# A pair's last 64 queries as one block-diagonal product, with single buffers for the transposed q and k

## The chip, the cores and the metric

The kernel runs on one core of one Trainium2 chip. The metric is the device time of one execution in microseconds. The kernel before takes 1670.19 us (median of 3 runs, 1670.05 to 1670.26). All arithmetic is in 32-bit floats, and the granted clock of TensorE in the profiled run was 0.997 of full speed.

## What is computed

Attention with a threshold, followed by a Fourier mixing block:

```python
# q, k, v: (8, 8, 576, 64)   batch, heads, sequence, head size
scores = q @ k.T / 8
thresh = max(scores, axis=-1) - tau
scores = where(scores >= thresh, scores, -1e9)
attn   = exp(scores - max) / (sum + 1e-9)
x      = attn @ v                     # as (8, 576, 512)
u      = x + real(fft(fft(x, axis=1), axis=2))
un     = (u - mean(u)) / sqrt(var(u) + 1e-6)
out    = u + relu(un @ w_ch1) @ w_ch2 # 512 -> 2048 -> 512
```

The change concerns `scores` only.

## The kernel before, in words

**Pairs and steps.** Two heads of a batch make a pair: head j of the pair lies on partitions 64j to 64j + 63. There are 32 pairs, four in a batch. The 576 queries are taken in five steps (`NT = 5`): steps 0 to 3 have 128 queries of each head, and step 4 has the last 64 of both heads, one head on each half of the partitions.

**Loading and transposing a pair.** `load_pair` (L124 to L147) brings q and k of a pair into one buffer `qk` of nine slots of 128 rows. Slots 0 to 3 hold the first 512 queries, slots 4 to 7 hold 512 keys, slot 8 holds the last 64 queries above 64 keys. The second head's keys are loaded in another order: the last 64 keys first, then 0 to 511, so its weights later lie where the product with v wants them. `prep_in_parts` (L389 to L416) transposes the nine slots on TensorE, in three parts. Part one: four transposes `pq`, then VectorE scales them into `qT` (L399). Part two: four transposes `pk`, then ScalarE copies them into `kT` (L406). Part three: one transpose `pt` of slot 8, then VectorE scales its q half into the end of `qT` (L410), copies its k half to the end of `kT` (L413), and the next pair's load is issued. `qT` and `kT` have two buffers each, so that the next pair can be transposed while the present one is still in use.

**Scores.** `scores(i)` (L422 to L448) fills PSUM tiles `sc`, of which there are two. In steps 0 to 3 it does four products over 64 rows each (L433), in step 4 five products of 64 rows by 64 columns (L444): both heads write to one tile, head 1's on the lower half of the partitions, and since head 1's keys are rotated by 64, its second half of the keys takes two products:

```python
for j, c, c0, k0, w in (
    (0, 0, 0, 0, HALF), (1, 0, 0, 64, HALF), (0, 1, 0, HALF, HALF),
    (1, 1, 0, 64 + HALF, 512 - HALF), (1, 1, 512 - HALF, 0, 64),
):
    hp = slice(64 * j, 64 * j + 64)
    nc.tensor.matmul(sc[0][hp, c, c0 : c0 + w], qT[hp, 512:S], kT[hp, k0 : k0 + w], ...)
```

**Softmax.** `softmax(i)` takes the maxima on VectorE (L461), the exponential on ScalarE (L469), the threshold and the sum on VectorE (L477), and the division (L492, L496). The weights are then transposed on TensorE (L541, L560), copied by ScalarE into `e_t` (L548 to L564) and multiplied with v (L589).

**What sets the order.** In the first two batches (pairs 0 to 7) every engine keeps the order of writing. The first batch also converts the first weight matrix from 64-bit input and fills TensorE with dummy products (`busy`, L112). The second converts the second weight matrix (L298 to L320, on VectorE, ScalarE and GpSimd in turn; `advance` takes the stages one by one) and starts the Fourier mixing and the channel products. From batch 3 on only TensorE keeps the order of writing, and a scheduler orders the other engines. There, `fill()` puts pieces of the Fourier mixing (L692 to L713) and of the channel products (L822, L848, L926, L1090), up to a budget per slot, between the pieces of attention: three slots a step. In batches 2 to 8 the next pair's preparation is called in step 3: in one go in batch 2 (`second_batch`), and in batches 3 to 8 one part at a time, before, between and after the transposes of the weights. In batch 1 it is called in step 4 (`step`). All products' PSUM tiles other than `sc` share four banks (tag `mm`).

Of the kernel before, what the change touches and what calls it, by code (L numbers as in the profile page):

```python
# [9 lines left out]
FP32 = mybir.dt.float32  # L10
INT32 = mybir.dt.int32
UINT32 = mybir.dt.uint32
ALU = mybir.AluOpType
# [34 lines left out]
def kernel(  # L48
# [12 lines left out]
    nc = tc.nc  # L61
    B, H, S, D = q.shape
# [3 lines left out]
    NPAIR = H // 2  # L66
# [3 lines left out]
    HALF = S // 2  # L70
# [12 lines left out]
    const = ctx.enter_context(tc.tile_pool(name="const", bufs=1))  # L83
    sb = ctx.enter_context(tc.tile_pool(name="sb", bufs=2))
# [39 lines left out]
    def load_pair(n, queue=nc.sync):  # L124
        b, p = n // NPAIR, PAIRS[n % NPAIR]
        hs = [2 * p + (j + p) % 2 for j in range(2)]

        qk = sb.tile([128, 9, 2, D], FP32, tag="qk", bufs=1, name="qk_in")
        for j, h in enumerate(hs):
            nc.sync.dma_start(  # L130
                out=qk[:, 0:4, j, :], in_=q[b, h, 0:512, :].rearrange("(t p) d -> p t d", p=128)
            )
            nc.sync.dma_start(out=qk[0:64, 8, j, :], in_=q[b, h, 512:576, :])


        h = hs[0]
        queue.dma_start(
            out=qk[:, 4:8, 0, :], in_=k[b, h, 0:512, :].rearrange("(t p) d -> p t d", p=128)
        )
        queue.dma_start(out=qk[64:128, 8, 0, :], in_=k[b, h, 512:576, :])  # L140
        h = hs[1]
        queue.dma_start(out=qk[0:64, 4, 1, :], in_=k[b, h, 512:576, :])
        rows = k[b, h, 0:512, :].rearrange("(t r p) d -> p r t d", r=2, p=64)
        queue.dma_start(out=qk[64:128, 4:8, 1, :], in_=rows[:, 0])
        queue.dma_start(out=qk[0:64, 5:8, 1, :], in_=rows[:, 1, 0:3])
        queue.dma_start(out=qk[64:128, 8, 1, :], in_=rows[:, 1, 3])
        loaded[n] = qk  # L147

    def load_v(n):
# [21 lines left out]
    for u in range(2):  # L171
        for j in range(2):
            nc.gpsimd.memset(v_in[u][64 - 64 * j : 128 - 64 * j, 8 + j, :], 0.0)
    eps = const.tile([128, 1], FP32, name="eps")
    nc.vector.memset(eps[:], 1e-6)

# [3 lines left out]
    q_scale = const.tile([128, 1], FP32, name="q_scale")  # L180
    nc.vector.tensor_scalar(
        out=q_scale[:], in0=tau_t[:], scalar1=0.0, scalar2=SCALE, op0=ALU.is_ge, op1=ALU.mult
# [3 lines left out]
        out=below[:], in0=tau_t[:], scalar1=0.0, scalar2=-3.0e38, op0=ALU.is_lt, op1=ALU.mult  # L186
# [3 lines left out]
        out=tau_pos[:], in0=tau_t[:], scalar1=0.0, scalar2=-1.0, op0=ALU.max, op1=ALU.mult  # L190
# [82 lines left out]
    hs = const.tile([128, NJ * GT], FP32, name="hs")  # L273
# [115 lines left out]
    def prep_in_parts(n):  # L389


        qk = loaded.pop(n)
        qT = sb.tile([128, S], FP32, tag="qT", name="qT")
        kT = sb.tile([128, S], FP32, tag="kT", name="kT")

        pq = ps.tile([128, 512], FP32, tag="mm", bufs=4, name="pq")
        for t in range(4):
            nc.tensor.transpose(pq[:, 128 * t : 128 * t + 128], qk[:, t, :, :], ident[:, :])
        nc.vector.tensor_scalar(  # L399
            out=qT[:, 0:512], in0=pq[:, :], scalar1=q_scale[:, :], scalar2=None, op0=ALU.mult  # L400
        )
        yield
        pk = ps.tile([128, 512], FP32, tag="mm", bufs=4, name="pk")
        for t in range(4):
            nc.tensor.transpose(pk[:, 128 * t : 128 * t + 128], qk[:, 4 + t, :, :], ident[:, :])
        nc.scalar.copy(kT[:, 0:512], pk[:, :])  # L406
        yield
        pt = ps.tile([128, 512], FP32, tag="mm", bufs=4, name="pt")
        nc.tensor.transpose(pt[:, 0:128], qk[:, 8, :, :], ident[:, :])
        nc.vector.tensor_scalar(  # L410
            out=qT[:, 512:S], in0=pt[:, 0:64], scalar1=q_scale[:, :], scalar2=None, op0=ALU.mult
        )
        nc.vector.tensor_copy(kT[:, 512:S], pt[:, 64:128])  # L413
        heads[n] = (qT, kT, v_in[n % 2])
        if n + 1 < B * NPAIR:
            load_pair(n + 1)  # L416
# [6 lines left out]
    def scores(i):  # L423
        n, t = divmod(i, NT)
        qT, kT = heads[n][0:2]

        nh = 2 if t < 4 else 1
        sc = [ps.tile([128, 2, 512], FP32, tag="sc", name=f"sc{j}") for j in range(nh)]
        if t < 4:
            for c in range(2):  # L430
                for j in range(2):
                    hp = slice(64 * j, 64 * j + 64)
                    nc.tensor.matmul(  # L433
                        sc[j][:, c, 0:HALF], qT[hp, 128 * t : 128 * t + 128],
                        kT[hp, HALF * c : HALF * (c + 1)], start=True, stop=True,
                    )
        else:

            for j, c, c0, k0, w in (
                (0, 0, 0, 0, HALF), (1, 0, 0, 64, HALF), (0, 1, 0, HALF, HALF),  # L440
                (1, 1, 0, 64 + HALF, 512 - HALF), (1, 1, 512 - HALF, 0, 64),
            ):
                hp = slice(64 * j, 64 * j + 64)
                nc.tensor.matmul(  # L444
                    sc[0][hp, c, c0 : c0 + w], qT[hp, 512:S], kT[hp, k0 : k0 + w],
                    start=True, stop=True, skip_group_check=True,
                )
        steps[i] = (sc, nh)  # L448

# [866 lines left out]
    def second_batch(i):  # L1316

        nonlocal budget
        n, t = divmod(i, NT)
        first = i - per_batch  # L1320
        if first != 1:
            scores(i)
        if first == 0:

            transposed_weights(i - 1)
        softmax(i, None, lambda: (advance(first - 1), advance(first - 1)))
        chunks.pop(first - 1, None)
        transfers(first)
        fold_more()
        if first == 0:  # L1330
            weighted_values(n - 1, 1)
            scores(i + 1)
            column_means(LAST)
            copy_mean(LAST)
            folds.append(fold_rows(n - 1))
            while folds:
                fold_more()
            load_v(n + 1)
            start_batch(0)
            mix(3)  # L1340
            mix(3)
        elif first == 1:
            mix(3)
            transposed_weights(i - 1)
            mix(2)
            mirrored(LAST)
            for c, eng in ((1, nc.vector), (3, nc.vector), (0, nc.gpsimd), (2, nc.gpsimd)):
                less_mean(eng, LAST, c)
            advance(first)
            advance(first)  # L1350
        elif first == 2:
            mix(2)
            transposed_weights(i - 1)
            mix(2)
            weighted_values(n, 0)
            advance(first)
            advance(first)
        else:
            fill()
            transposed_weights(i - 1)  # L1360
            advance(first)
            advance(first)
            fill()
            if t == 3:
                prep_pair(n + 1)
            fill()
            if t == 2:
                weighted_values(n, 0)
            if t == 0:
                weighted_values(n - 1, 1)  # L1370
                folds.append(fold_rows(n - 1))
                load_v(n + 1)
        if first == 16:
            fold_halves(1)
        if first < 3:
            budget += 3 * per_slot
# [7 lines left out]
    by_hand.close()  # L1384
    ctx.enter_context(tc.manual_schedule(engines={mybir.EngineType.PE}))

    for i in range(2 * per_batch, total + 1):


        if i < total:  # L1390
            scores(i)
        n, t = divmod(i, NT)
        if t > 2:
            fold_more()
        nothing = iter(())
        prep = prep_in_parts(n + 1) if t == 3 and n + 1 < B * NPAIR else nothing
        weights = weights_in_parts(i - 1)
        next(prep, None)
        fill()
        next(weights, None)  # L1400
        fill()
        next(weights, None)
        next(prep, None)
        if i < total:
            softmax(i)
        fill()
        next(prep, None)
        if t == 2:
            weighted_values(n, 0)
        if t == 0:  # L1410
            while folds:
                fold_more()
            weighted_values(n - 1, 1)
            folds.append(fold_rows(n - 1))
            if n % NPAIR == 0:
                while folds:
                    fold_more()
            if n + 1 < B * NPAIR:
                load_v(n + 1)
        if i % per_batch == 0:  # L1420
            start_batch(i // per_batch - 1)
# [49 lines left out]
```

## Time and profile before

| | |
|---|---|
| time, median of 3 | 1670.19 us |
| span of the profiled run | 1669.6 us |
| TensorE busy | 1621.8 us, 97% |
| VectorE, ScalarE, GpSimd busy | 69%, 50%, 35% |
| L433, scores of steps 0 to 3 | 1024 passes, 168.6 us busy |
| L444, scores of step 4 | 320 passes, 38.2 us busy |
| L398, L405, L409, transposes of a pair | 288, 48.5 us busy |
| L399 / L406 / L410 / L413, one instruction | 741 / 592 / 274 / 211 ns |

A group's line gives the line of the code, engine, operation, result and operands, the shape, how many, their busy time, and the idle time of the engine before them with what ended it. A 32-bit product is recorded as two passes, so the 160 products of L444 count as 320; a transpose counts once. Matmuls are pipelined and their ends are modelled, so busy time adds up overlaps: what a group costs is better read from the distance between starts in the timeline. "PEld" is the loading of weights, which can run beside products. In the timeline the bracket at a line's end is the idle time of the engine ahead of it and what released it.

### The profile page before, as it was taken

How to read it: one execution, taken by the hardware profiler on the slowest of the kernel's cores; microseconds unless marked ns; L12 is line 12 of the kernel's file. 1: busy time of each engine (PE TensorE's matmuls, PEld its weight loads, DVE VectorE, ACT ScalarE, POOL GpSimd, SP SyncE). 2: the span in 40 equal slices, each digit the busy share in tenths (PEclk: the TensorE clock that was granted, in tenths of full speed). 3: DMA queues.
4: the chain of work that ended last, by engine and by line, in shares of the span. 5: the costliest groups of instructions: out<-in, count | busy, mean ns of one | idle time of the engine just before them, and what ended most of it. 6: DMA issues, size and time to landing. Idle time of an engine off the chain costs nothing.

```text
span 1669.6 us, 28885 instructions
## 1 busy us (share of the span) xinstructions
PE 1621.8 (97%) x10826; PEld 1273.6 (76%) x10826; DVE 1146.0 (69%) x2518; ACT 837.9 (50%) x1817; POOL 581.9 (35%) x779
## 2 busy tenths in 40 slices
PE   8998899999999999999999999999999999999998
PEld 4555555577887888878888778887878788889998
DVE  6887785567757686857566858686677768664454
ACT  5775675544455454545354546454646455532111
POOL 5674562041321442134332143213242244215232
PEclk9999999999999999999999999999999999999999
DMA  5423222100010101000101010111001010000000
GB/s 157 121 55 110 73 73 56 30 20 21 19 39 15 29 15 42 23 28 8 28 22 35 10 34 15 42 22 29 22 16 42 22 32 4 14 1 13 14 13 13
DMA packets 130384, 57.48 MB, mean 34 GB/s; under 512 B 121123, under 2 KB 121125, under 8 KB 130246
## 3 DMA queue, kind: packets, MB, share of 16 engines
q1 hardware_dynamic: 128854, 55.35, 12.3%
q8 instruction: 86, 1.41, 0.4%
q14 instruction: 52, 0.43, 0.1%
q10 hardware_dynamic: 1392, 0.30, 0.1%
HBM read 46.02 MB, written 9.44 MB: 33 GB/s over the span
## 4 chain that ended last, share of the span: by engine, by line
PE 76%; DVE 15%; ACT 7%; issue 2%; POOL 1%; DVEq 0%; ACTq 0%; POOLq 0%
PE ph L926 23%; PE po L1090 18%; PE pv L589 8%; PE sc L433 7%; PE pw L560 5%; PE po L848 3%; DVE e L477 3%; DVE neg L461 2%; ACT e L469 2%; DVE hs L1051 2%; PE sc L444 2%; PE ph L822 1%; PE py L692 1%; PE pa L709 1%; PE pn L782 1%
## 5 line engine op out<-in xcount | busy, mean ns | idle before, releaser
L469 ACT ACTIVATE e<-sc,neg 128x576 f32<-128x576 f32 x288 | 212.6, 738 | 238.1 <-DVE neg L461 237.4
L461 DVE TENSOR_REDUCE neg<-sc 128x1 f32<-128x576 f32 x288 | 206.2, 750 | 171.4 <-PE sc L433 158.5
L477 DVE SCALAR_TENSOR_TENSOR e<-sc,thr,e 128x576 f32<-128x576 f32 x288 | 229.7, 811 | 57.5 <-ACT thr L473 54.2
L1090 PE MATMUL po<-w,hs 128*128 128x256 f32 x1024 | 246.3, 383 | 0.5 <-DVE u L804 0.5
L1090 PEld LDWEIGHTS po<-w,hs 128*128 128x128 f32 x1024 | 186.0, 190 | 33.6 <-issue 11.2
L926 PE MATMUL ph<-u_t,w 128*128 128x128 f32 x1536 | 187.2, 276 | 0.0
L926 PEld LDWEIGHTS ph<-u_t,w 128*128 128x128 f32 x1536 | 178.7, 192 | 4.4 <-issue 3.3
L560 PE MATMUL pw<-ident,e 128*128 128x128 f32 x1152 | 169.5, 274 | 10.4 <-ACT kT L406 2.7
L562 ACT COPY e_t<-pw 128x512 f32<-128x512 f32 x256 | 148.9, 596 | 59.8 <-PE pw L560 59.3
L433 PE MATMUL sc<-kT,qT 64*128 64x288 f32 x1024 | 168.6, 429 | 6.8 <-DVE e L477 6.0
L560 PEld LDWEIGHTS pw<-ident,e 128*128 128x128 f32 x1152 | 134.2, 141 | 29.3 <-issue 4.3
L935 DVE TENSOR_TENSOR hs<-ph,hs 128x512 f32<-128x512 f32 x160 | 106.9, 685 | 71.4 <-PE ph L926 46.8
L433 PEld LDWEIGHTS sc<-kT,qT 64*128 64x128 f32 x1024 | 93.2, 186 | 69.3 <-issue 37.2
L926 PE MATMUL ph<-t_u,s_w 128*128 128x128 f32 x1024 | 126.0, 276 | 2.2 <-POOL t_u L900 1.8
L804 DVE SCALAR_TENSOR_TENSOR u<-po,rstd,u 128x256 f32<-128x256 f32 (+1 forms) x164 | 75.4, 484 | 73.8 <-PE po L1090 71.9
L926 PEld LDWEIGHTS ph<-t_u,s_w 128*128 128x128 f32 x1024 | 119.4, 192 | 5.3 <-issue 2.6
L1090 PE MATMUL po<-hs,s_tile 128*128 128x256 f32 x512 | 122.1, 382 | 0.0
L496 ACT ACTIVATE e<-e,den 128x576 f32<-128x576 f32 x96 | 75.0, 781 | 67.4 <-DVE den L489 66.7
L1090 PEld LDWEIGHTS po<-hs,s_tile 128*128 128x128 f32 x512 | 93.6, 190 | 13.6 <-issue 2.1
L943 ACT ACTIVATE hs<-hs 128x512 f32<-128x512 f32 x112 | 69.4, 631 | 63.9 <-DVE hs L935 63.9
L622 POOL TENSOR_TENSOR half<-x 128x287 f32<-128x287 f32 x48 | 40.4, 862 | 125.5 <-ACT x L595 70.7
L1086 POOL TENSOR_TENSOR hs<-hs,s_tile 128x512 f32<-128x512 f32 x32 | 42.3, 1323 | 117.5 <-PE po L1090 113.8
(199 smaller groups left out, 2905.8 us busy)
## 6 DMA issues: line engine op xcount, KB each, us to landing
hs<-in_moe_w_ch_dram SPq DMA_DIRECT2D x23, 512.0 KB, 4.4
out_dram<-u SPq DMA_DIRECT2D x36, 256.0 KB, 2.2
qk_in<-in_q_dram SPq DMA_DIRECT2D x64, 128.0 KB, 2.3
v_in<-in_v_dram SPq DMA_DIRECT2D x64, 128.0 KB, 2.4
qk_in<-in_k_dram SPq DMA_DIRECT2D x31, 128.0 KB, 2.5
w<-in_moe_w_ch_dram SPq DMA_DIRECT2D x6, 512.0 KB, 8.4
qk_in<-in_k_dram SPq DMA_DIRECT2D x31, 64.0 KB, 2.3
stage<-in_moe_w_ch_dram SPq DMA_DIRECT2D x3, 512.0 KB, 3.8
```

Of the source, the lines that this page charges most:

```text
L433: nc.tensor.matmul(sc[j][:, c, 0:HALF], qT[hp, 128 * t : 128 * t + 128], kT[hp, HALF * c : HALF * (c + 1)], start=True, stop=True,)
L461: nc.vector.tensor_reduce(out=neg[:, j : j + 1], in_=sc[j][:, :, 0:HALF], axis=AXIS_XY, op=ALU.max, negate=True,)
L469: nc.scalar.activation(out=ej, in_=sc[j][:, :, 0:HALF], func=ACT.Exp, bias=neg[:, j : j + 1], scale=1.0)
L477: nc.vector.scalar_tensor_tensor(out=ej, in0=sc[j][:, :, 0:HALF], scalar=thr[:, j : j + 1], in1=ej, op0=ALU.is_ge, op1=ALU.mult, accum_out ...
L496: nc.scalar.activation(out=e[:, S : 2 * S], in_=e[:, S : 2 * S], func=ACT.Copy, scale=den[:, 1:2])
L560: nc.tensor.transpose(pw[:, c, :], e[:, c0 : c0 + 128], ident[:, :])
L562: nc.scalar.copy(e_t[:, 4 * j : 4 * j + 4, qs], pw[:, :, :])
L589: nc.tensor.matmul(pv[64 * j : 64 * j + 64, 0:m], vt[:, 2 * c + j, :], e_t[:, 4 * j + c, 0:m] if c < 4 else ends[:, 0:m], start=(c == 0), ...
L804: nc.vector.scalar_tensor_tensor(out=u, in0=product, scalar=self.rstd[:, t : t + 1], in1=u, op0=ALU.mult, op1=ALU.add,)
L926: nc.tensor.matmul(banks[name][:, 128 * q : 128 * q + 128], left[c][:, 512 * part + 128 * q : 512 * part + 128 * q + 128], right[c], start ...
L935: nc.vector.tensor_tensor(out=to, in0=bank, in1=to if other is None else other, op=ALU.add)
L1090: nc.tensor.matmul(bank[:, 0 : DM // 2], left[p], right[p], start=start and p == 0, stop=p == NK - 1, skip_group_check=True,)
```

## The change

The scores of step 4 become two products over all 128 rows. A constant tile `q_ends` of 128x128, cleared once, holds head 0's last 64 queries in its upper left quarter and head 1's in its lower right quarter. Multiplied with both heads' keys it gives both heads' scores on their own halves of the partitions, in one full-array product per half of the keys. For this both heads' keys have to stand in the same, natural order: the second head is loaded like the first, with two transfers in place of four. `kT` gets 64 columns more in front, where head 1's last 64 keys are copied a second time, so that steps 0 to 3 can still read head 1's keys rotated. `qT` loses its last 64 columns, and `qT` and `kT` have one buffer each. Since the preparation now writes over what step 4's scores read, parts two and three move behind those scores: in batch 2 the whole preparation is called in step 4, and in batches 3 to 8 part one stays in step 3 and parts two and three go to step 4.

```diff
-        h = hs[0]
-        queue.dma_start(out=qk[:, 4:8, 0, :], in_=k[b, h, 0:512, :]...)
-        queue.dma_start(out=qk[64:128, 8, 0, :], in_=k[b, h, 512:576, :])
-        h = hs[1]
-        queue.dma_start(out=qk[0:64, 4, 1, :], in_=k[b, h, 512:576, :])
-        rows = k[b, h, 0:512, :].rearrange("(t r p) d -> p r t d", r=2, p=64)
-        queue.dma_start(out=qk[64:128, 4:8, 1, :], in_=rows[:, 0])
-        queue.dma_start(out=qk[0:64, 5:8, 1, :], in_=rows[:, 1, 0:3])
-        queue.dma_start(out=qk[64:128, 8, 1, :], in_=rows[:, 1, 3])
+        for j, h in enumerate(hs):
+            queue.dma_start(out=qk[:, 4:8, j, :], in_=k[b, h, 0:512, :]...)
+            queue.dma_start(out=qk[64:128, 8, j, :], in_=k[b, h, 512:576, :])
...
+    q_ends = const.tile([128, 128], FP32, name="q_ends")
+    nc.gpsimd.memset(q_ends[:, :], 0.0)
...
-        qT = sb.tile([128, S], FP32, tag="qT", name="qT")
-        kT = sb.tile([128, S], FP32, tag="kT", name="kT")
+        qT = sb.tile([128, 512], FP32, tag="qT", bufs=1, name="qT")
...
-        nc.scalar.copy(kT[:, 0:512], pk[:, :])
+        kT = sb.tile([128, D + S], FP32, tag="kT", bufs=1, name="kT")
+        nc.scalar.copy(kT[:, D : D + 512], pk[:, :])
         yield
         pt = ps.tile([128, 512], FP32, tag="mm", bufs=4, name="pt")
         nc.tensor.transpose(pt[:, 0:128], qk[:, 8, :, :], ident[:, :])
-        nc.vector.tensor_scalar(out=qT[:, 512:S], in0=pt[:, 0:64], scalar1=q_scale[:, :], ...)
-        nc.vector.tensor_copy(kT[:, 512:S], pt[:, 64:128])
+        nc.vector.tensor_copy(kT[64:128, 0:D], pt[64:128, 64:128])
+        nc.vector.tensor_copy(kT[:, 512 + D : D + S], pt[:, 64:128])
+        for j in range(2):
+            hp = slice(64 * j, 64 * j + 64)
+            nc.vector.tensor_scalar(out=q_ends[hp, hp], in0=pt[hp, 0:64], scalar1=q_scale[hp, :], ...)
...
-                    hp = slice(64 * j, 64 * j + 64)
+                    hp, k0 = slice(64 * j, 64 * j + 64), D * (1 - j)
-                        kT[hp, HALF * c : HALF * (c + 1)], start=True, stop=True,
+                        kT[hp, k0 + HALF * c : k0 + HALF * (c + 1)], start=True, stop=True,
...
-            for j, c, c0, k0, w in (...):          # the five products above
+            for c in range(2):
                 nc.tensor.matmul(
+                    sc[0][:, c, 0:HALF], q_ends[:, :], kT[:, D + HALF * c : D + HALF * (c + 1)],
...
-            if t == 3:                              # batch 2
+            if t == 4:
                 prep_pair(n + 1)
...
-        prep = prep_in_parts(n + 1) if t == 3 and n + 1 < B * NPAIR else nothing
+        if t == 3 and n + 1 < B * NPAIR:            # batches 3 to 8
+            prep = prep_in_parts(n + 1)
         weights = weights_in_parts(i - 1)
-        next(prep, None)
+        if t > 2 and prep is not None:
+            next(prep, None)
         fill()
         next(weights, None)
         fill()
         next(weights, None)
-        next(prep, None)
+        if t == 4 and prep is not None:
+            next(prep, None)
         if i < total:
             softmax(i)
         fill()
-        next(prep, None)
```

## The prediction

> **What bounds the kernel now.** I read the page's shares and slices first, then busy time by stage, then the group of the line that goes (its instructions and what they wait for), then the timeline of TensorE around one of its executions, and last the timelines around the loads of a new pair. The page:
>
> ```profile
> PE 1621.8 (97%) x10826; PEld 1273.6 (76%) x10826; DVE 1146.0 (69%) x2518; ACT 837.9 (50%) x1817; POOL 581.9 (35%) x779
> ...
> PE 76%; DVE 15%; ACT 7%; issue 2%; POOL 1%; DVEq 0%; ACTq 0%; POOLq 0%
> ```
>
> TensorE is busy 97% of the span; the chain that ended last still runs 22% through VectorE and ScalarE. Where each holds shows by stage (TensorE, weight loads, VectorE, ScalarE, GpSimd, busy us with counts; granted clock; DMA):
>
> ```profile
> 20.00:150.00 130.00, 120.05 (x666) 70.72 (x665) 107.85 (x260) 92.75 (x214) 74.55 (x90) 0.98 0.41 119
> 150.00:310.00 160.00, 147.91 (x791) 89.08 (x790) 120.06 (x276) 100.08 (x228) 77.54 (x96) 0.99 0.21 56
> 310.00:1460.00 1150.00, 1134.59 (x7961) 920.56 (x7960) 802.86 (x1779) 592.58 (x1265) 350.96 (x470) 1.00 0.10 24
> ```
>
> From 310 to 1460 us (batches 3 to 8, 24 pairs) TensorE is 98.7% busy: time taken off it there is time off the span. In the first batch (to 150 us) it is filled up with dummy products (L112), so its time is worth nothing; the chain of VectorE and ScalarE paces it. The second batch (150 to 310 us) is mixed: 12 us of TensorE idle, in pieces of 0.3 to 2.5 us, with VectorE, ScalarE and GpSimd in written order.
>
> One execution of the product that goes, on TensorE, with what stands before and after it (start us, us):
>
> ```profile
> 1001.86 0.60 PE L560 MATMUL pw<-ident,e 128*128 128x128 f32 x4
> 1002.30 0.60 PE L405 MATMUL pk<-ident,qk_in 128*128 128x128 f32 x4
> 1002.74 1.95 PE L926 MATMUL ph<-u_t,w 128*128 128x128 f32 x16
> 1004.52 0.27 PE L409 MATMUL pt<-ident,qk_in 128*128 128x128 f32 x1
> 1004.73 1.20 PE L444 MATMUL sc<-kT,qT 64*64 64x288 f32 x10
> 1005.85 2.05 PE L926 MATMUL ph<-u_t,s_w 128*128 128x128 f32 x16
> 1007.74 0.27 PE L541 MATMUL pe<-ident,e 128*128 128x128 f32 x1
> ```
>
> Ends are modelled, so I use distances between starts. L444 takes 1.12 us until the next start. A single transpose takes 0.11 us from start to start (four in 0.44, L405), but pt to L444 takes 0.21: 0.10 lost going in. Sixteen passes of L926 take 1.78 us after a transpose (1002.74 to 1004.52) and 1.89 after L444: 0.11 lost coming out. All 32 executions look alike (1.12 or 1.13 us).
>
> **What the Trainium skill says.** "TensorEngine Tiling (Array Packing)", Tiling Modes: changing the tiling mode drains TensorE, and different tiles run in parallel. The trace agrees: the 0.10 and 0.11 us on the two sides of the 64x64 products, which transitions among 128x128 instructions don't have; and the ten passes, 2304 columns in all, take 1.12 us, where the full array needs 1.73 us for 2048 (below), so the two quadrants do overlap. "TensorE: Matmul & The Clock Gate", Part 1, Architectural detail: TensorE can pull weight loads ahead, ScalarE and VectorE are strict first-in, first-out. The trace shows both: weight loads start before the product ahead of them has ended, and ScalarE's copies into kT stand behind whatever was issued first.
>
> **The change, part by part.**
>
> *The product.* Five 64x64 products (ten passes) become two 128x128 ones with the weights q_ends (four passes of 288 columns, 1152 in all). The nearest rows are L1090's: eight passes of 256 columns from 1034.43 to 1036.16, 1.73 us, 0.845 ns a column; just after a 64-row product it is 1.82 us (1029.06 to 1030.88), 0.89 ns. So the new product takes 0.97 us (1.02 at worst), and no mode changes on its two sides. A gain of 1.12 + 0.10 + 0.11 - 0.97 = 0.36, of which I keep 0.34 since neighbours differ; 0.21 if only the ends go, 0.10 if only the body. 24 pairs x 0.34 = 8.2 us. Batch 1: 0. Batch 2 is reckoned as a whole below.
>
> *K and q in natural order, fewer transfers.* Two transfers of k fewer per pair, the same bytes. Each takes SyncE about 0.6 us to issue, but they start a pair ahead and DMA is 10% busy: worth 0, hidden behind four steps of TensorE. At the start of the kernel the transposes wait for the dummy products (L112 runs up to 9.85 us) and not for k, so 0 there too.
>
> *Copies.* VectorE does two copies into kT and two scalings into q_ends, where it did one copy (0.21 us, L413) and one scaling (0.27, L410). I take about 0.2 us each, 0.85 against 0.48: +0.4 us a pair, or 12 us in all on an engine that is 69% busy. Worth 0 while it's not waited for; clearing q_ends is one memset at the start, on GpSimd, hidden likewise.
>
> *One buffer each for qT and kT, so k's transposes move behind step 4's scores.* In batches 3 to 8, pt now stands one slot of filling work (1.8 to 3.2 us) before the new pair's first scores. VectorE must have ended its queue and done two copies by then. From the trace of before, shifted by the moves: pt ends 6.1 to 8.7 us after step 4's scores, the instructions that the changed order puts ahead of the copies end at 5.0 to 9.9 us, the copies take 0.45 more, and the scores come at 7.8 to 11 us. The slack is 0.2 us at the least (the pair after 849 us), 0.4 after 539 and 585, over 1 elsewhere. So 0 there, with a risk. Behind the waiting copies in VectorE's queue stand additions to hs and step 0's maxima; TensorE needs these some 3 us later.
>
> *Batch 2, four pair boundaries.* Here all engines keep the written order, and the changed order on TensorE has the nine transposes and then at once the next scores (no filling work is placed between them at any of the four). The best case is the kernel's start:
>
> ```profile
> 9.85 0.60 PE L398 MATMUL pq<-ident,qk_in 128*128 128x128 f32 x4
> ...
> 10.92 0.59 ACT L406 COPY kT<-pk 128x512 f32<-128x512 f32 x1 [3.94 <-PE pk L405]
> ...
> 11.34 0.21 DVE L413 COPY kT<-pt 128x64 f32<-128x64 f32 x1
> ...
> 11.56 1.24 PE L433 MATMUL sc<-kT,qT 64*128 64x288 f32 x8 [0.57 <-DVE kT L413]
> ```
>
> 1.71 us from pq to the scores with idle engines; the transposes are 0.97 of it, so 0.74 is bare waiting. It is worse with a full queue. At 250 us ScalarE runs, in the order of writing, ahead of where kT's copy now stands:
>
> ```profile
> 256.58 0.66 ACT L306 ACTIVATE w<-w 128x512 f32<-128x512 int32 x1
> 257.11 0.74 ACT L309 ACTIVATE u_t<-u_t,shift 128x512 int32<-128x512 int32 x1
> 257.72 0.69 ACT L312 ACTIVATE stage<-stage 128x512 f32<-128x512 int32 x1
> 258.28 0.75 ACT L469 ACTIVATE e<-sc,neg 128x576 f32<-128x576 f32 x1
> ```
>
> There, step 4's scores start 1.1 us earlier (249.4, no transposes ahead), TensorE is through the transposes at 255.5, ScalarE through the conversions at 257.3 and kT's copy at 257.9: the scores start at 258.0 against 255.62 before, 2.4 later. TensorE's wait of 1.0 us at 261.25 (for e_t) then falls away: net +1.4. In the same way: boundary at 174 us, scores 2.5 later, of which some 0.9 comes back from waits of 0.31 (181.4) and 1.50 (201.8): +1.6. Boundary at 211 us, where two sets of conversions (four VectorE, six ScalarE instructions) stand ahead: scores 6 us later, but the 2.51 us wait at 226.5 and 1.4 inside the product after it go: +2.5. Boundary at 284 us, only copies ahead: +0.9. Sum +6.4 us, the faster product included. From below: 4 x 0.74 less 4 x 0.34, +1.6; from above, with nothing given back, +11.8.
>
> Sum: 1670.2 - 8.2 + 6.4 = 1668.4 us.
>
> **Rivals.** *B, batch 2 costs only its lower end:* other waits swallow the delay. 12 us of idle there speaks for it; written order on three engines against it. 1670.2 - 8.2 + 1.6 = 1663.6. *C, slower: a wait takes the removed one's place.* If VectorE is later than I read it, kT comes too late at the 23 later boundaries as well; 0.4 us each is +9: 1677.6. For it: slacks of 0.2 to 0.4 us in the tightest and VectorE instructions stretched to 1.5 us at times (L492, L301); against it: over 1 us in most. *D, slower: the full product saves no mode change* because its neighbours lose as much at their waits: 24 x 0.10 = 2.4 in place of 8.2 gives 1674.2. Against it: all transitions among 128x128 instructions that I looked at cost nothing.
>
> **How the numbers follow.** My case 0.42, B 0.30, C 0.16, D 0.12. My case spreads over 1665 to 1671.5, a quarter of it below the bound of 0.2% (1666.9): faster 0.30 + 0.10 = 0.40; same 0.32 and a little of C and D, 0.36; slower 0.24. Range: low is B with up to 2 us more from step 3's lighter load (waits for qT and kT at L560 total 4.6 us), 1661.5; high is D and the lower part of C, 1675.
>
> **What would show it.** Each new product taking 0.95 to 1.02 us between starts, with no 0.1 us on its sides: else D. Waits of TensorE for kT at the first scores of a pair, 1 to 7 us each, in 170 to 300 us only: if small there, B; if they run on past 310 us, C. The stage 310 to 1460 us should end about 8 us shorter, the stage 150 to 310 about 6 longer. I'd be wrong if the scheduler's new order of VectorE or GpSimd makes waits in places that have nothing to do with the pair's boundary.

## The result, and the profile after

The changed kernel takes 1677.83 us (median of 4 runs, 1677.02 to 1680.12), the kernel before, beside it, 1670.21 us (1670.05 to 1670.26). The ratio is 1.0048, 95% interval 1.0031 to 1.0065. The change makes the kernel 7.6 us slower. The prediction, 1668.4 us with a range to 1675.0, was wrong: on the wrong side, and above its range.

The page of the kernel after, its shares and the engines of the chain that ended last:

```profile
PE 1617.8 (96%) x10634; PEld 1278.8 (76%) x10634; DVE 1165.7 (69%) x2582; ACT 838.8 (50%) x1817; POOL 582.1 (35%) x780
...
PE 72%; DVE 17%; ACT 8%; issue 2%; POOL 1%; DVEq 0%; ACTq 0%; POOLq 0%
```

TensorE has 192 passes fewer, but the chain now runs 28% of the span outside it, where it was 24%. The stages (columns as before: TensorE, weight loads, VectorE, ScalarE, GpSimd, granted clock, DMA):

```profile
20.00:150.00 130.00, 119.08 (x654) 71.94 (x653) 108.99 (x262) 92.52 (x211) 74.64 (x92) 0.99 0.40 118
150.00:310.00 160.00, 139.68 (x713) 85.34 (x712) 113.11 (x263) 92.39 (x211) 76.87 (x93) 0.95 0.21 54
310.00:1460.00 1150.00, 1132.47 (x7787) 921.12 (x7786) 819.62 (x1829) 593.50 (x1265) 349.11 (x468) 1.00 0.10 24
```

Two things stand out. In the stage of batch 2 (150 to 310 us) TensorE does 713 passes instead of 791, and its granted clock is 0.95, where it was 0.99. In the stage of batches 3 to 8, where I had expected 8 us, VectorE has 16.8 us more work (802.86 before), though the added copies are only some 13 us of it.

One new product in the timeline of TensorE (start us, us), the counterpart of the excerpt shown of before:

```profile
1100.92 1.95 PE L923 MATMUL ph<-u_t,w 128*128 128x128 f32 x16
1102.71 1.14 PE L441 MATMUL sc<-kT,q_ends 128*128 128x288 f32 x4
1103.68 0.60 PE L401 MATMUL pk<-ident,qk_in 128*128 128x128 f32 x4
1104.12 1.95 PE L923 MATMUL ph<-u_t,w 128*128 128x128 f32 x16
```

L441 takes 0.97 us to the next start, the sixteen passes ahead of it 1.79, as between two full products, and the transposes behind it the usual 0.44. So nothing is lost on its sides any more, and the gain of 0.34 us a pair is there. It must be lost again elsewhere.

Where, the starts of each pair's first scores tell: their difference from the kernel before, taken over a batch, is what the batch gained or lost. This table is worked out from the timelines of the profiled executions, one of each kernel; a minus sign means less time than before. An execution's own spread in a batch is up to some 2 us (the version with two buffers was profiled twice: batch 4 gave -1.5 and +0.8), and the first scores of the kernel start up to 1.6 us apart. The profiled execution of the kernel after took 1680.12 us, 2.3 more than the median, and that of before 1671.41, 1.2 more.

| after less before, us | batch 1 | batch 2 | batches 3 to 8 |
|---|---|---|---|
| forecast | 0 | +6.4 | -8.2 |
| kernel after | -0.8 | +12.3 | -1.0 |

Batch 2, at its second pair boundary, on TensorE:

```profile
217.32 0.66 PE L394 MATMUL pq<-ident,qk_in 128*128 128x128 f32 x4 [2.28 <-ACT recs L545]
217.82 0.60 PE L401 MATMUL pk<-ident,qk_in 128*128 128x128 f32 x4
218.25 0.27 PE L407 MATMUL pt<-ident,qk_in 128*128 128x128 f32 x1
223.39 2.29 PE L435 MATMUL sc<-kT,qT 64*128 64x288 f32 x8 [4.86 <-ACT kT L403]
225.61 4.91 PE L819 MATMUL ph<-u_t,w 128*128 128x384 f32 x8
```

and on ScalarE, the last of six conversions and the copy that TensorE waits for:

```profile
222.23 0.63 ACT L308 ACTIVATE hs<-hs 128x512 f32<-128x512 int32 x1
222.77 0.56 ACT L403 COPY kT<-pk 128x512 f32<-128x512 f32 x1
```

The wait for kT stands where it was forecast: the scores come 13.2 us after those of step 4 (210.24), the working gave 12.1. Two things were not forecast. The transposes ahead of it have themselves waited 2.28 us, for ScalarE's copy of `recs`. And behind it the scores take 2.22 us to the next start, where eight such passes take 1.17, and the eight passes of L819 take 4.74, where they take 2.6 to 2.7: TensorE works at half speed for some 6.4 us. The clock that the trace records is at half from 219.6 to 229.8 us, part of it in the wait; over the slice of 20 us around it that makes 0.74 (it is 0.91 in the slices of the waits at 178 and 264 us, and 1.00 in the five others of batch 2):

```profile
210.00:230.00 20.00, 12.86 (x50) 8.12 (x49) 14.91 (x33) 12.65 (x26) 9.43 (x9) 0.74 0.30 82
```

The waits by their totals:

```profile
PE sc L435 <- ACT kT L403: 10.1, 5, 4.9
PE sc L435 <- DVE e L474: 6.6, 17, 1.3
```

Five waits for kT, 0.5 to 4.9 us, of which four stand at batch 2's boundaries (the fifth is at the start of the kernel, 0.6 us), and none past 310 us. So rival C, whose mechanism was a kT that comes too late at all the later boundaries, is not what happened; that its 1677.6 us is near to the time is luck.

### The profile page after: what moved, and what is told of

Read it like the earlier page. It is cut to its first block, busy times and chain, and to the rows that moved or that the text cites. A ratio compares the mean times of both kernels' runs of the same rounds, so it can differ in the third digit from the quotient of the medians.

```text
span 1678.0 us, 28469 instructions
## 1 busy us (share of the span) xinstructions
PE 1617.8 (96%) x10634; PEld 1278.8 (76%) x10634; DVE 1165.7 (69%) x2582; ACT 838.8 (50%) x1817; POOL 582.1 (35%) x780
## 4 chain that ended last, share of the span: by engine, by line
PE 72%; DVE 17%; ACT 8%; issue 2%; POOL 1%; DVEq 0%; ACTq 0%; POOLq 0%
PE ph L923 22%; PE po L1087 18%; PE pv L586 7%; PE sc L435 7%; PE pw L557 5%; DVE e L474 3%; PE po L845 3%; DVE neg L458 3%; ACT e L466 2%; PE ph L819 2%; DVE hs L1048 2%; PE sc L441 2%; PE py L689 1%; PE pa L706 1%; PE pn L779 1%
## 5 line engine op out<-in xcount | busy, mean ns | idle before, releaser
L435 PE MATMUL sc<-kT,qT 64*128 64x288 f32 x1024 | 173.0, 436 | 16.9 <-ACT kT L403 10.1
L619 POOL TENSOR_TENSOR half<-x 128x287 f32<-128x287 f32 x48 | 40.5, 864 | 127.3 <-ACT x L592 70.7
L489 DVE TENSOR_SCALAR e<-e,den 128x576 f32<-128x576 f32 x120 | 81.2, 676 | 3.4
```

The lines of the kernel that those rows point to most:

```text
L435: nc.tensor.matmul(sc[j][:, c, 0:HALF], qT[hp, 128 * t : 128 * t + 128], kT[hp, k0 + HALF * c : k0 + HALF * (c + 1)], start=True, stop=True,)
L489: nc.vector.tensor_scalar(out=e[:, 0:S], in0=e[:, 0:S], scalar1=den[:, 0:1], scalar2=None, op0=ALU.mult)
```

## The experiments

All ratios are to the kernel before, run beside. The net of a batch is what it takes more or less than in the kernel before, worked out as above from one profiled execution; the times are medians of several runs.

**Two buffers, the old place.** The product, its four copies and the order of the keys stay; kT and q_ends get a second buffer, and the transposes go back behind step 3 in all batches (the loop of batches 3 to 8 is that of the kernel before):

```diff
-    q_ends = const.tile([128, 128], FP32, name="q_ends")
+    q_ends2 = [const.tile([128, 128], FP32, name=f"q_ends{u}") for u in range(2)]
...
-        kT = sb.tile([128, D + S], FP32, tag="kT", bufs=1, name="kT")
+        kT = sb.tile([128, D + S], FP32, tag="kT", bufs=2, name="kT")
...
-            if t == 4:
+            if t == 3:
                 prep_pair(n + 1)
```

> The block-diagonal product and the natural order are kept; kT and q_ends have two buffers each, and the preparation stands where the kernel before had it (all in step 3). Theory: the single kT is what makes the kernel slower, twice. In batch 2 it makes TensorE wait for kT and lose its clock (pair 4's first scores to pair 8's: 12.3 us longer than before, 6.4 forecast); in batches 3 to 8 the moved copies delay VectorE at the start of each batch and eat the 8.2 us that the product saves. With two buffers both go: 1661 to 1663 us. Rival, the additional copies themselves (1.0 us of VectorE a pair in place of 0.5) eat the gain wherever they stand: batch 2 is cured but batches 3 to 8 gain 2 us at most, 1667 to 1669 us.

Measured 1662.04 us, 0.9956 (0.9942 to 0.9971). Run again later, in more rounds:

> The version with two buffers once more, in more rounds, as the base of the next run and to tell its size: 1661 to 1664, both theories.

1662.80 us, 0.9959 (0.9945 to 0.9972). Both times it is the theory's number, and faster than both kernels. Its stages 150 to 310 and 310 to 1460 us:

```profile
150.00:310.00 160.00, 147.40 (x765) 88.77 (x764) 124.75 (x287) 102.74 (x233) 76.65 (x93) 1.00 0.21 56
310.00:1460.00 1150.00, 1135.19 (x7890) 930.02 (x7889) 819.86 (x1837) 595.62 (x1273) 352.74 (x470) 1.00 0.10 24
```

Batch 2 has no loss (-1.7 us, what four faster products and lighter steps give) and the clock stays at 1.00. So the product itself is good, and its extra copies can be borne in this place: what costs comes with the move of the transposes.

**The place alone.** The kernel before, with its five products, its copies and its double buffers, and only the transposes moved as in the change:

```diff
-            if t == 3:
+            if t == 4:
                 prep_pair(n + 1)
...
-        prep = prep_in_parts(n + 1) if t == 3 and n + 1 < B * NPAIR else nothing
+        if t == 3 and n + 1 < B * NPAIR:
+            prep = prep_in_parts(n + 1)
...
-        next(prep, None)
+        if t == 4 and prep is not None:
+            next(prep, None)
```

> The kernel before with its five small products, its two copies and its double buffers; only the preparation is called where the changed kernel calls it (step 4 in batch 2, parts two and three in step 4 from batch 3 on). Theory (the place costs): no product gain, about +12 us in batch 2 and +7 in batches 3 to 8, 1687 to 1690 us. Rival (the additional copies cost in batches 3 to 8, not the place): +12 in batch 2 and at most +2 later, 1682 to 1684 us.

1684.34 us, 1.0088 (1.0073 to 1.0103), 0.3 us above the rival's range. Batch 2 loses 10.0 us: its loss comes with the place. Batches 3 to 8 lose 1.7 in the profiled execution, but that one is the fastest of the four, 2.4 us below the median.

The times say what the place costs in all. With the old product it is 15.0 us (1669.37 to 1684.34); with the new one, the changed kernel less the version with two buffers, it is a ratio of 0.0089 to 0.0092, some 15 us as well. And the product with its copies gains some 7 us in either place (0.9956 or 0.9959 against 1, and 1.0048 against 1.0088). So the times show no loss that needs the new place and the copies together: it comes out at under 1 us, with an uncertainty of some 4.5.

**No idle stretch in batch 2.** The changed kernel, with 2, 5, 2 and 0 dummy products written into the gaps at the four boundaries:

```diff
             if t == 4:
                 prep_pair(n + 1)
+                keep_warm({4: 2, 9: 5, 14: 2, 19: 0}[first])
```

> The changed kernel with dummy products (2, 5, 2 and 0 of 128x512) between the transposes and the next scores at the four pair boundaries of batch 2, so that TensorE has work while it waits for kT. The waits for kT stay. Theory: of the 12.3 us lost there, some 6 are passes at half clock after waits of 1.8 to 4.9 us; kept busy, the clock stays and 4 to 6 us come back: 1672 to 1674 us. Rival: the clock after the waits costs little, since VectorE and ScalarE set the pace there: 1677 to 1678 us.

1676.20 us, 1.0041 (1.0026 to 1.0056), between the two numbers, and not clear of the changed kernel's 1.0048 (1.0031 to 1.0065). The second boundary on TensorE:

```profile
220.30 4.50 PE L122 MATMUL pd<-ones 128*128 128x512 f32 x10
225.34 1.24 PE L445 MATMUL sc<-kT,qT 64*128 64x288 f32 x8 [0.54 <-ACT kT L413]
226.51 2.85 PE L829 MATMUL ph<-u_t,w 128*128 128x384 f32 x8
```

Scores and product are back at full speed (1.17 and 2.68 us), and the clock is 1.00 in all slices of batch 2. TensorE does useless work and the kernel doesn't get slower for it: in the profiled executions batch 2 loses 7.8 us in place of 12.3 in the changed kernel, or of 9.6 and 9.9 in two others that have its order there. By these the slow clock is 2 to 4.5 us of the loss, and the rest is the waiting itself; the medians, 6.8 and 7.6 us above the kernels before beside them, are too near to each other to confirm the size.

**The transposes ahead of the conversions.** The changed kernel; in batch 2 the preparation is written before the two stages of conversion, so that ScalarE's copy into kT doesn't stand behind them:

```diff
             transposed_weights(i - 1)
+            if t == 4:
+                prep_pair(n + 1)
             advance(first)
             advance(first)
             fill()
-            if t == 4:
-                prep_pair(n + 1)
```

> The changed kernel, single buffers kept; in batch 2 the preparation at step 4 is written ahead of the conversions of the second weight matrix instead of behind them, so that ScalarE copies kT before its six conversions. Theory: these conversions are what kT's copy waits for; TensorE's waits for kT fall to under 1 us each, the clock stays, and most of the 12 us come back: 1668 to 1671 us. Rival: the conversions, later now, delay the softmax of the next step by as much: 1675 to 1678 us.

1677.78 us, 1.0044 (1.0030 to 1.0059): missed, the rival's number. Batch 2 still loses 7.7 us. The wait for kT is nearly gone, but another has come in its place, 1.8 to 2.8 us at each boundary:

```profile
176.62 0.66 PE L401 MATMUL pk<-ident,qk_in 128*128 128x128 f32 x4 [1.75 <-ACT recs L545]
```

The transposes now follow directly on those of the weights; what ended their waits was ScalarE's copy of `recs` out of one of the four shared PSUM banks. Behind step 4's scores they wait on one side or the other. Behind step 3's they don't (in the version with two buffers TensorE waits neither ahead of the transposes nor for kT there).

**Batch 2 cured, the rest as changed.** Two buffers, the old place in batch 2 only (the edits of the first diff, with the loop of batches 3 to 8 left as the change has it):

> Two buffers for kT and q_ends, and in batch 2 the transposes of q and k back behind step 3; in batches 3 to 8 everything stands as in the changed kernel. Theory (batch 2 loses by the place of the transposes there; in batches 3 to 8 a second loss of its own eats the product's 8 us, since the transposes and four copies now stand at the end of a pair's VectorE work): batch 2 is cured, batches 3 to 8 still net only -1 to -2 us, total 1667 to 1669. Rival (the loss of batches 3 to 8 is a consequence of the single buffers, or of batch 2's lateness carried on): batches 3 to 8 net -5 to -6, total 1662 to 1664.

1668.06 us (21 runs, 1663.98 to 1670.23), 0.9986 (0.9979 to 0.9992), the theory's number. Batch 2 is cured. Batches 3 to 8 net -3.2 us, which is neither theory's, in an execution that is the fastest of the 21 and 4.1 us below their median. From the version with two buffers this one differs by the place in batches 3 to 8 alone, and its time is some 5 us longer (0.9986 against 0.9956 and 0.9959, clear of noise). So there is a second loss, independent of batch 2. Half speed is not all of it: among runs with the same granted clock over the whole span, 0.998, those of this version average 1665.7 us (4 runs) and those of the version with two buffers 1661.6 (3 runs).

What the place costs in batch 2 is then some 10.4 us (1.0048 less 0.9986). If it is the same with the old product, the place alone costs 4 to 5 us in batches 3 to 8 by the medians, an estimate, where the one trace of it shows 1.7.

**Where in batches 3 to 8.** In the profiled execution of the changed kernel the pairs within a batch gain their 0.3 to 0.4 us; it is lost at the first pair of a batch, most plainly in batches 7 and 8 (+1.3 us each from the first pair to the second). There VectorE folds the rows of the last pair's result (L619, two additions of two SBUF operands) and mixes them (L670). VectorE in the changed kernel, batch 7:

```profile
1123.18 1.73 DVE L619 TENSOR_TENSOR half<-x 128x287 f32<-128x287 f32 x2
...
1129.35 1.54 DVE L670 SCALAR_TENSOR_TENSOR f<-sums,factors 128x304 f32<-128x304 f32 x1
```

GpSimd at the same time:

```profile
1122.75 1.47 POOL L1083 TENSOR_TENSOR hs<-hs 128x512 f32<-128x512 f32 x1 [9.41 <-DVE s_tile L1083]
1128.97 1.59 POOL L1083 TENSOR_TENSOR s_tile<-s_tile,hs 128x512 f32<-128x512 f32 x1 [4.74 <-PE po L1087]
```

Each of the two VectorE entries lies on a GpSimd one. Such an overlap is called a meeting below. The same work takes 0.82 and 0.53 us where GpSimd is idle (the next experiment). The Trainium skill has this: "SBUF — State Buffer", SBUF: two separate sides, says that VectorE and GpSimd share one pair of ports under an exclusive lock, and that a VectorE operation with two SBUF inputs is fully blocked while a GpSimd operation that reads SBUF holds it. The trace agrees: L670, which came second, ends 0.3 us after the GpSimd instruction that it met (1130.89 and 1130.56). GpSimd's instructions are longer too, 1.47 and 1.59 us, where they take 1.27 in the next experiment. TensorE then waits for what stands behind on VectorE:

```profile
1131.78 1.94 PE L435 MATMUL sc<-kT,qT 64*128 64x288 f32 x8 [0.27 <-DVE e L474]
```

The eight passes take 1.87 us in place of 1.17, since the second tile comes later still. From the transposes at 1126.45 to the work behind these scores at 1133.65 it is 7.2 us; in the next experiment 5.7.

**The two scalings on ScalarE.** The changed kernel with 0.56 us a pair less on VectorE:

```diff
-            nc.vector.tensor_scalar(
-                out=q_ends[hp, hp], in0=pt[hp, 0:64], scalar1=q_scale[hp, :], scalar2=None,
-                op0=ALU.mult,
+            nc.scalar.activation(
+                out=q_ends[hp, hp], in_=pt[hp, 0:64], func=ACT.Copy, scale=q_scale[hp, :]
```

> The changed kernel with the two scalings into q_ends (0.28 us each on VectorE) done by ScalarE. Theory (in batches 3 to 8 VectorE's extra copies at the pair's end put the additions, denominators and the multiplications by e behind them, which TensorE then waits for): with 0.56 us a pair taken off VectorE at that place batches 3 to 8 net -4 to -6 in place of -1, total 1673 to 1675; batch 2 as bad as in the changed kernel. Rival (VectorE's copies are not it; the late place of the transposes on TensorE and ScalarE is): batches 3 to 8 stay at 0 to -1.5, or worse as ScalarE's exponentials wait behind two more instructions, total 1677 to 1680.

1675.68 us (1674.65 to 1678.93), 1.0039 (1.0027 to 1.0052): between the two numbers, and not clear of the changed kernel's 1.0048, so the times don't decide. In the trace batch 2 is nearly as bad as in the changed kernel (+9.9), batch 1 loses 1.7 us, and batches 3 to 8 net -5.6 us, as the theory said. Of the 4.6 us over the changed kernel, 3.1 are in batches 7 and 8, and 1.6 in batch 5, where another cause is at work (below). The same place in batch 7, VectorE:

```profile
1121.65 0.82 DVE L618 TENSOR_TENSOR half<-x 128x287 f32<-128x287 f32 x2 [2.07 <-ACT x L591]
...
1126.91 0.53 DVE L669 SCALAR_TENSOR_TENSOR f<-sums,factors 128x304 f32<-128x304 f32 x1
```

and GpSimd:

```profile
1119.65 1.27 POOL L1082 TENSOR_TENSOR hs<-hs 128x512 f32<-128x512 f32 x1 [4.20 <-DVE s_tile L1082]
1127.43 1.27 POOL L1082 TENSOR_TENSOR s_tile<-s_tile,hs 128x512 f32<-128x512 f32 x1 [6.51 <-PE po L1086]
```

The fold starts as long after its scores as in the changed kernel (0.6 us), for it waits for ScalarE; but GpSimd's instruction, which waits for VectorE's L1082, is over before it. In the changed kernel VectorE comes to the new pair's first maxima 3.5 us after their scores (2.0 here), and the whole queue, with what GpSimd waits for, is later by that. A meeting is not dear in itself: in this kernel L678 meets GpSimd at 1129.92 us and takes 1.47 us, and TensorE waits only 0.34 behind it. VectorE's order also differs between the two kernels.

**The two scalings done twice.** The changed kernel with 0.56 us a pair more on VectorE at that place:

```diff
-        for j in range(2):
+        for j in (0, 1, 0, 1):
             hp = slice(64 * j, 64 * j + 64)
```

> The changed kernel with the two scalings into q_ends done twice over, 0.56 us more of VectorE a pair at the same place, same result. Theory (VectorE's copies there eat the product's gain): batches 3 to 8 net +2 to +5 in place of -1, total 1681 to 1684. Rival (VectorE's copies there are hidden): batches 3 to 8 still about -1, total 1677 to 1679.

1678.41 us (1678.06 to 1682.20), 1.0056 (1.0044 to 1.0069): the rival's number. Batches 3 to 8 net -1.0, as in the changed kernel. So it isn't VectorE's time that TensorE pays for, us by us. In this kernel too, `half` and `f` of L619 and L670 take 756 and 862 ns on the mean (750 and 867 in the changed kernel, 567 and 527 with the scalings on ScalarE). The meetings are the same in both kernels, and a little more work ahead of them changes nothing.

**A meeting made on purpose.** The version with two buffers, with two useless GpSimd additions written ahead of the last pair's fold. Nothing is added to, or changes its order on, TensorE, VectorE and ScalarE, and the two traces have the same sequence on each of the three:

```diff
+        if last and b >= 2:
+            for c0 in (1, 257):
+                nc.gpsimd.tensor_tensor(
+                    out=unused[:, :], in0=x[:, c0 : c0 + 256], in1=x[:, c0 : c0 + 256], op=ALU.add
+                )
```

> The version with two buffers, and ahead of the fold of each batch's last pair (two VectorE additions with both inputs in SBUF, batches 3 to 8) two useless GpSimd additions of 256 columns that read the same tile and write a tile that nobody reads: no instruction more on TensorE, VectorE or ScalarE, and none in another order. Theory (the rest of the product's gain goes where VectorE's instructions with two SBUF inputs meet a GpSimd instruction: one of the two is held, and TensorE waits for what stands behind it): the fold's pair of additions goes from some 0.7 to 1.3 us or more, and each of the six batches loses 0.5 to 1.3 us, 1665 to 1670. Rival (such meetings are hidden behind TensorE's work): within 1 us of the base.

1668.52 us (21 runs, 1666.22 to 1671.05), 0.9994 (0.9988 to 1.0001), against 1662.80 of its base beside it: 5.7 us lost, by 12 instructions of 0.8 us on an engine that is 35% busy. Half speed doesn't explain it: among runs with a granted clock of 0.998 the averages are 1668.3 us (7 runs) and 1662.1 (2 runs). Nor does GpSimd's own lateness: the one wait of TensorE for GpSimd in batches 3 to 8, 1.8 us for `t_u`, is the same in both traces. The groups of VectorE from 310 to 1460 us (busy us, mean ns), of the base:

```profile
L622 DVE TENSOR_TENSOR half<-x 128x287 f32<-128x287 f32 x10 | 6.5, 687 | 4.8 <-ACT x L595 4.7
L627 DVE TENSOR_TENSOR f<-half 128x143 f32<-128x143 f32 x20 | 4.7, 295 | 0.0
L673 DVE SCALAR_TENSOR_TENSOR f<-sums,factors 128x304 f32<-128x304 f32 x5 | 2.6, 523 | 0.0
```

and with the additions:

```profile
L628 DVE TENSOR_TENSOR half<-x 128x287 f32<-128x287 f32 x10 | 8.1, 852 | 4.8 <-ACT x L596 4.7
L633 DVE TENSOR_TENSOR f<-half 128x143 f32<-128x143 f32 x20 | 7.2, 420 | 0.0
L679 DVE SCALAR_TENSOR_TENSOR f<-sums,factors 128x304 f32<-128x304 f32 x5 | 3.6, 727 | 0.0
```

VectorE is held 5.1 us longer in these three groups, and batches 3 to 8 lose 6.2 us in the profiled execution, 1.1 to 1.2 of it in each of batches 6, 7 and 8, and 1.8 in batch 5 (another cause, below). Even L673, which the additions don't touch, is longer: once VectorE is late, it also meets the next GpSimd instruction. The theory's time was hit. In the fold it was wrong on the size: 0.7 us is the mean of one of its two additions and not of the pair, the pair rose from 1.4 to 1.7 us, and the four additions behind it took most of the rest.

**Two buffers and the scalings on ScalarE.** Both edits together, in the hope of a still faster kernel:

> The version with two buffers and the transposes behind step 3 everywhere (1662.0, batches 3 to 8 net -6.3), with the scalings into q_ends on ScalarE. Theory: the rest of the product's 8.2 us comes with VectorE's copies, so batches 3 to 8 net -7 to -8.2, total 1660 to 1661.5. Rival (at that place nothing waits for VectorE's copies, and ScalarE pays for two more): 1662 to 1665.

1668.37 us (13 runs, 1667.33 to 1671.33), 0.9992 (0.9984 to 1.0001): slower than with the scalings on VectorE, beyond even the rival's 1662 to 1665. Batch 1 loses 4.6 us in its profiled execution (waits of scores for e of 1.65 and 1.81 us, and a clock of 0.91 and 0.83 between 20 and 60 us), and its batch 5 has TensorE at half speed behind a wait, as told below. Whether ScalarE's exponentials, behind two more instructions, make the waits in batch 1 in every execution was not followed further; 13 runs, none below 1667 us, say that the loss is not one execution's.

What each order nets, us against before, from the profiled executions, and how far each execution lies from its kernel's median:

| kernel | batch 2 | batches 3 to 8 | execution less median |
|---|---|---|---|
| after | +12.3 | -1.0 | +2.3 |
| place alone | +10.0 | +1.7 | -2.4 |
| no idle stretch | +7.8 | -1.5 | +1.1 |
| transposes ahead of conversions | +7.7 | +1.0 | +1.6 |
| scalings on ScalarE | +9.9 | -5.6 | 0.0 |
| scalings twice | +9.6 | -1.0 | 0.0 |
| batch 2 cured | -1.7 | -3.2 | -4.1 |
| two buffers (two executions) | -1.7, -1.7 | -6.4, -5.3 | -0.7, -1.0 |
| two buffers, meeting made | -1.7 | +0.9 | +2.3 |
| two buffers, scalings on ScalarE | -0.6 | -3.5 | +3.0 |

So a net that differs from another's by 2 or 3 us proves little alone.

One more term is in these nets. In batch 5 TensorE waits 1.8 us for GpSimd's `t_u` (at 749 us in the kernel before), in every kernel. In some executions its clock then falls to 0.83 over ten us: in the changed kernel, with dummy products, with the transposes first and with the scalings twice, where batch 5 nets +0.9 to +1.5 us. With batch 2 cured and with the scalings on ScalarE it stays at 1.00 there, and the batch nets -0.8 and -0.7. The version with two buffers shows both, in its two executions (-0.9 and -2.0). Batch 4 has the same: of these two executions only the second has half speed there, at 520 us (+0.8 against -1.5). So this is half speed again, by execution and not by kernel as far as these runs tell, and 1.1 to 2.3 us each time.

**What the traces show of half speed.** Half speed is granted for 3.41 us, or for two or three times as long, and within a trace all these stretches start on one grid of 3.41 us. Apart from the first 15 us and the last 20 us, the twelve traces have 40 such starts. In the grid window of 3.41 us just ahead of each, TensorE was busy for 19 to 69% of the time. Of the windows at full speed, all nine that were busy for less than 41% were followed by half speed, and none of those above 69%; between the two it goes both ways. So the length of one wait doesn't decide alone: it counts how the waits fall into a window of this grid, which lies differently in every execution. The waits of 2.28 and 4.86 us above share one: it is 35% busy, and half speed starts at its end.

## Why the prediction was wrong

By the traces the forecast for batch 2 was 5.9 us too low, and that for batches 3 to 8 promised 7.2 us too much. Two steps failed: the clock behind the waits of batch 2, which was taken to stay at full speed, and the moved parts in batches 3 to 8, which were put at nothing.

*The product: right.* 0.97 us between starts and nothing lost on its sides, as worked out. Rival D falls; so does B, since batch 2 cost more than the forecast and not less.

*Batch 2, the waits: right in place and nearly in size.* Apart from the kernel's start, TensorE waits for kT at the four boundaries of this batch only. From step 4's scores to the next pair's first the working gives 8.5, 12.1 and 8.6 us at the first three; measured are 8.1, 13.2 and 9.0. With the clock kept up, the batch loses 7.8 us, near the 6.4 forecast.

*Batch 2, the clock: the step that was missing.* The working added waits and took full speed for granted behind them. The Trainium skill has the mechanism ("TensorE: Matmul & The Clock Gate", Part 1: TensorE's clock falls to half after an idle window of about 3.4 us); here the window need not be idle throughout: half speed came with waits of 4.9, but also of 2.3 and 1.8 us, after windows that were 35, 32 and 39% busy. The sign of it was in an excerpt that I had read: the product behind the wait of 2.51 us in the kernel before, 1.4 us too long, which I booked as waiting "inside the product" that the change would give back:

```profile
226.53 3.83 PE L589 MATMUL pv<-e_t,v_rev 128*64 128x320 f32 x16 [2.51 <-ACT e_t L564]
230.20 0.70 PE L589 MATMUL pv<-ends,v_rev 128*64 128x320 f32 x4
```

The sixteen passes take 3.67 us, where sixteen such passes at 261.25 us take 2.20. It was TensorE at half clock (from 226.1 to 229.5 us, 0.91 in that slice of before), and what the change gave back there it took at three other boundaries. By the profiled executions this is 2 to 4.5 us of the miss.

*Copies, "worth 0 while it's not waited for": wrong in the trace, not shown by the times.* The copies' size was wrong by a little: 0.23, 0.23 and two of 0.28 us, 1.01 in place of 0.85 us a pair. Their delay was compared with slack at the boundary only, where it did hold: kT was in time at all 23. In the trace of the changed kernel VectorE then comes 1.5 us later to the first pair of batches 7 and 8 than with the scalings on ScalarE, its folds meet GpSimd's instructions, and TensorE loses 1.5 us there. Taking the scalings off VectorE brought 3.1 of the missing 7.2 us back in batches 7 and 8. Another 1.6 us of the 7.2 is half speed in batch 5. That such a meeting costs TensorE time is shown: made on purpose in an otherwise fast kernel, it cost 1.1 to 1.2 us a batch in batches 6 to 8, and 5.7 us in all by the times. That the copies cause the meetings is argued from one trace: the time didn't move clear of noise with the scalings on ScalarE, nor with the scalings done twice.

*Moved parts in batches 3 to 8, "0, with a risk": the second step that failed.* The risk was reckoned as a kT that comes too late, and it never does. But the place in these batches, which is all that sets the version with batch 2 cured apart from that with two buffers, costs some 5 us of time, and the move in all costs some 15 us with the old copies as with the new. The forecast's last sentence named "waits in places that have nothing to do with the pair's boundary" as what would make it wrong, and the stretched instructions were seen (in rival C), but as noise and not as a cost that depends on timing.

The account from the trace: -0.8 in batch 1, +12.3, -1.0, and -1.6 from the first scores' own start, is +8.9; the two profiled spans differ by 8.4. What stays open: what more than its busy share decides whether a window brings half speed; the last 2 us or so of the missing 7.2; how the 5 us of batches 3 to 8 divide between late copies, meetings and half speed, and what the move costs there without the copies; and how the scheduler's order of VectorE, which differs between these kernels beside the added work, shares in the meetings. No run held that order fixed and took away the copies.

## What to carry to other kernels

A wait of some 2 us on TensorE can be paid twice: allow for the product behind it at half speed, and look in the trace of before for products that are too long just after a wait. Keep the buffer that lets a transfer or a transpose run ahead: here the buffers saved put, in batch 2, nine transposes and six copies at the one place where every queue was full, and the move cost some 15 us in all, twice what the better product brings; with the buffers kept, the same product makes the kernel 0.4% faster. And "off the critical path" is a statement on one engine: a delay there can move another engine's instructions onto shared ports, so read VectorE's and GpSimd's timelines together at the tightest place before writing 0.

## What the runs showed of the hardware

- TensorE's half speed after waits: eight passes of 288 columns 2.2 in place of 1.17 us, eight of 384 columns 4.74 in place of 2.6 to 2.7. It came with waits of 2.3, 4.9 and 1.8 us, in stretches that start at 178.6, 219.6 and 263.9 us, but not with each wait of 2 us: after 1.75 us at 177 us in the version with the transposes first four transposes took 0.50, near their usual 0.44.
- These stretches last 3.41 us or two or three times that, start on one grid of 3.41 us in each trace, and follow a window of that grid in which TensorE was busy for 19 to 69% of the time (40 stretches, twelve traces).
- With useless products in such gaps the kernel was not slower (1.0041 against 1.0048), and the clock stayed at 1.00 in batch 2.
- VectorE beside GpSimd: two additions of 287 columns with both operands in SBUF take 0.82 us alone and 1.73 with a GpSimd addition running; a fold of 304 columns 0.53 and 1.54.
- A copy of 64 columns from PSUM took 0.21 to 0.23 us on VectorE, whether on 64 or on 128 partitions; a scaling took 0.27 to 0.28 us there, and 0.31 on ScalarE on 64 partitions.
